# Two transformer layers on one core: earlier loads ahead of attention, idle steps and bursts in the fronts, dummy matmuls at the start

## The chip, the core and the metric

The kernel runs on one NeuronCore of a Trainium2 chip. The metric is the device time of one execution in microseconds (us). A core has TensorE (PE, matmuls; its weight loads are listed apart as PEld), VectorE (DVE), ScalarE (ACT), GpSimd (POOL) and SyncE (SP), each with an instruction stream of its own that runs in order. Streams wait for one another by semaphores. DMA transfers are issued here from SP's stream and, a few, from ACT's; an issue that must wait for data holds up everything behind it in that stream.

## What is computed

Two identical layers, each an attention block and an MLP, over 2048 rows of 640 numbers, 32 heads of 20, 1536 hidden units, all in float32:

```python
def _A_ref(x, wqkv, wo):
    q, k, v = split of x @ wqkv into 32 heads of 20
    p = softmax(einsum("bhqd,bhkd->bhqk", q, k) * 20 ** -0.5)
    return (p @ v, heads joined) @ wo

def _B_ref(x, w1, b1, w2, b2):
    h = relu(x @ w1 + b1)
    return (h * h) @ w2 + b2

x = A_x
for _ in range(2):
    x = x + _A_ref(_layernorm(x), A_wqkv, A_wo)
    x = x + _B_ref(_layernorm(x), B_w1, B_b1, B_w2, B_b2)
```

## The kernel before

**Numbers in two parts.** Operands of the projections are split in a high and a low part of PE's fast float32 format (`F32R`), and each product is three matmuls: high by high, high by low, low by high (`THREE`, L325). The high part is a cast, the low part a subtraction. `split_to` (L256) does this on ACT and DVE, `split_on_pool` (L261) copies on ACT and splits on POOL.

**Stages of a layer.** `layer` (L1223) runs `qkv`, then `attention`, then four row blocks through the output projection and the MLP. A row block is 512 rows (`NQB` = 4 blocks).

**Fronts.** `front` (L438) is a generator: it loads the four 128-row tiles of a block, takes their statistics (`stats`, L241: DVE, then two small operations on POOL), normalises them (`normalise`, L253, on DVE), and transposes them on PE (L453), four transposes for each of the five 128-column chunks, each chunk followed by its split into a tile `xnT`. Every `yield` ends one step: rows, four statistics, four normalisings, five transposed chunks, 14 steps. Block 0 of layer 1 has its own `first_front` (L463), whose transposes are L473. In layer 1 the steps of blocks 1 to 3 are pulled by `qkv`, with the next block's rows requested at the last normalising (`fronts`, L493). In layer 2 (`second`, L1276) blocks 0 to 2 are pulled by the last row block of layer 1's MLP, through `side()`, two steps after each of its units of PE work from the eighth on (L1268), and block 3 by layer 2's `qkv`.

**Projections.** `qkv` (L783) goes through 40 units of 15 steps each (`UNITS`: first four column blocks of queries and keys for every row block, then the other six), then 16 value units (`v_unit`, L416) of 30 steps. A step is one full matmul in the first four units (L353) and two half matmuls later (L358 and, 22 steps behind, L367). After every step `between` (L901) counts: every fourth step pulls one step of the fronts, and at a pace written by hand it puts in a pair of score tiles (L561) whose row maxima DVE takes (L587 for plain ones; L595 on ACT and L602 on DVE for two tiles at once). These maxima are needed before the softmax. `STEPS` and `DOUBLE` say after which unit which maxima are asked for; `tiles` (L827) loads the keys and queries of an item and of the two after it. Results go to memory as `d_qk` and `d_v`, and come back regrouped by heads: one `load_k` or `load_q` is six DMAs of 80 KB (`load_k` of a kept tile two more, from the constant `d_one`). Stores are issued 10 to 16 steps late (`later`, L820), the value stores 12.

**Around the end of `qkv`** all loads stand in SP's stream in the order in which the code reaches them. After value unit 12 come k(0,0) to k(0,3) and q(1); after unit 13 k(3,0) to k(3,3), q(12) and q(13). k(g,c) is the c-th quarter of the keys of the g-th group of four heads, q(t) the queries of block t = 4g + row block.

**Attention.** `attention` (L985) runs 32 blocks of 16 tiles of 128 keys. `ORDERS` writes out by hand how scores (L657), exponentials on ACT (L664), remaining maxima (L561, from block 12 on) and the products with the values (L669) alternate on PE. For each block the maxima are turned into two rows, stored and loaded beside q (`mrows`, `mrows_load`, L634).

**Buffers.** 42 slots of 4 KB per partition (`slot`, L67) hold all large tiles, a smaller pool the row tiles; the eight PSUM banks are handed out in rings (`ps_q` has five). `sums_t` and `d_one` hold constants; `sums_t` is used once, at the end of each layer's attention (L695).

Of the kernel before, what the change touches and what calls it, by code (L numbers as in the profile page):

```python
# [39 lines left out]
def tile_layers(  # L40
# [397 lines left out]
    def front(tb, x_src, bank):  # L438

        rows = [row_tile(x_src, tb * 4 + i) for i in range(4)]  # L440
        yield
        mvs = []
        for x in rows:
            mvs.append(stats(x))
            yield
        for x, mv in zip(rows, mvs):
            normalise(nc.vector, x, mv)
            yield
        res = []
        for k in range(KD):  # L450
            dst = bank("xt")
            for i in range(4):
                nc.tensor.transpose(  # L453
                    dst[:, i * P : (i + 1) * P], rows[i][:, k * P : (k + 1) * P], ident
                )
            t = slot([P, 2, QB], F32R, "xnT")
            (split_on_pool if tb > 1 else split_to)(t[:, 0, :], t[:, 1, :], dst)
            res.append(t)
            if k == KD - 1:
                xt_[tb] = res  # L460
            yield

    def first_front(x_src):  # L463


        rows = [row_tile(x_src, i) for i in range(4)]
        yield
        mvs, dsts = [], [ps_all("xt") for _ in range(KD)]

        def turn(i):  # L470
            normalise(nc.vector, rows[i], mvs[i])
            for k in range(KD):
                nc.tensor.transpose(  # L473
                    dsts[k][:, i * P : (i + 1) * P], rows[i][:, k * P : (k + 1) * P], ident
                )

        for i in range(4):
            mvs.append(stats(rows[i]))
            if i:
                turn(i - 1)  # L480
            yield
        turn(3)
        yield
        res = []
        for dst in dsts:
            t = slot([P, 2, QB], F32R, "xnT")
            split_to(t[:, 0, :], t[:, 1, :], dst)
            res.append(t)
            if len(res) == KD:
                xt_[0] = res  # L490
            yield

    def fronts(steps):  # L493


        for n, f in enumerate(steps):
            for m, _ in enumerate(f):
                if m == 7 and n + 1 < len(steps):
                    next(steps[n + 1])
                yield  # L500

# [281 lines left out]
    def qkv(first, x_src, rest):  # L783
# [22 lines left out]
        for k in range(KD if first else w_v.n):  # L806
            n = len(UNITS) - 7 + k
            if first:
                at(early, n - 2, lambda k=k: raws.append(raw_rows(wqkv[:, 2 * D :], k)))
                at(late, n, lambda k=k: w_v.put(  # L810
                    raws.pop(0), k * 4, k * 4 + 2, 2, nc.scalar.copy, pool_lo
                ))
            else:
                at(early, len(UNITS) - 4 + k // 2, lambda k=k: w_v.load(k))

        def begin(when, n):
            for f in when.pop(n, ()):
# [83 lines left out]
        def between(cost):  # L901
            state["pace"] -= cost
            if state["pace"] <= 0:
                state["pace"] += some()
            settle(state["n"])
            state["n"] += 1
            if state["n"] % 4 == 0:
                next(rest, None)

        run = Halves(between)  # L910
# [24 lines left out]
        for tt in range(NKT):  # L935

            def end(store, tt=tt):
                later(store, 12)
                if tt % 4 == 3:
                    del xt_[tt // 4]  # L940

            v_unit(tt, run, end)
            if first:
                w_v.save_full(1)
            if tt == 10:
                load_v(0, 0)
            if tt == 12:
                for c in range(4):
                    assert (0, c) not in k_t
                    load_k(0, c, True)  # L950
                load_q(1)
            if tt == 13:
                for c in range(4):
                    load_k(3, c, True)
                for qb in range(2):
                    load_q(3 * NQB + qb)
        while run.behind:
            run.catch()
        while double or twos or begun:
# [263 lines left out]
    def layer(first, x_a, x_m, x_e, front_0, ahead):  # L1223
        qkv(first, x_a, front_0)
        if first:
            dma(nc.sync, b1_t, b1.rearrange("(f p) -> p f", p=P))
            dma(nc.sync, b2_t, b2.partition_broadcast(P))
        xs = []
        attention(first, x_a, xs)
        steps = []  # L1230
# [28 lines left out]
        for qb in range(NQB):  # L1259
# [5 lines left out]
                steps.extend([None] * 6 + [step, both, both, step, step, step, step, both])  # L1265
            elif ahead:
                some = lambda: [next(ahead, None) for _ in range(2)]
                steps.extend([None] * 7 + [some] * 21)  # L1268
            xnt = mlp(qb, xnt, x_m, x_e, side, rows if qb + 1 < NQB else None)
            if qb + 1 < NQB:  # L1270
                all_steps()
# [15 lines left out]
    def begin_first():  # L1287
        f = first_front(x_in)
        next(f)
        for pos in range(FIRST):  # L1290
            raws.append(raw_cols(wqkv, ORDER[pos]))
        steps = [front(tb, x_in, ps_q) for tb in (1, 2, 3)]
        for _ in range(5):
            next(f)
# [8 lines left out]

    ones = slot([2, QB], F32, "ones")
    nc.vector.memset(ones, 1.0)
    for p in range(2):
        dma(nc.scalar, d_one[:, p, :], ones)
    for h in range(4):
        r = 32 * h + DH
        dma(nc.scalar, sums_t[r : r + 1, 32 * h : 32 * h + 32], d_one[0, :1, :32])  # L1310
    ahead = second()
    layer(True, x_in, d_x[0], d_x[1], begin_first(), ahead)
    layer(False, d_x[1], d_x[2], x_out, ahead, None)
# [28 lines left out]
```

## Time and profile before

| | us |
|---|---|
| median of 3 runs | 3647.99 |
| lowest and highest | 3645.79, 3652.98 |
| the profiled execution, its own time | 3648.68 |
| its span, first to last instruction | 3646.9 |
| PE busy | 3589.5 |
| ACT busy | 2701.7 |
| DVE busy | 2648.6 |
| POOL busy | 865.5 |

The rows quoted below come from one profiled execution. Times run from the start of the span. Line numbers are those of the kernel before. A row of the timeline has start, length, engine, line, operation, what it writes and reads, the count where equal instructions were merged, and in brackets how long the engine stood before it and for what. A row of waits has the waiting work, what it waited for, the sum, the number of times and the longest. A row of windows has the window, its length, then the busy time and the number of instructions of PE, PEld, DVE, ACT and POOL, then the clock that the throttle granted PE (1.00 is full), the DMA engines' busy share and GB/s.

In this execution layer 1's `qkv` fills the time to about 348, its attention that to 1415, its output projection and MLP that to 1841; in layer 2 the same borders lie at about 2160 and 3233.

### The profile page before, as it was taken

What the parts mean: (1) busy time and instruction counts of PE and PEld (TensorE: products, weight loads), DVE (VectorE), ACT (ScalarE), POOL (GpSimd) and SP (SyncE); (2) the same over time, 40 slices, a digit from 0 to 9 for tenths busy, and PEclk for the clock granted to TensorE, in tenths of its full rate; (3) what the DMA queues carried; (4) which work ended last, traced back from release to release, by engine and by line L of the source; (5) the groups of instructions that cost most, each with busy time, mean ns of one, the idle gap of its engine ahead of it and who ended that gap; (6) DMA issues with size and microseconds to landing.
All of it is one profiled execution on the core that took longest, in us unless ns stands there. A gap on an engine that the chain in (4) does not pass through costs nothing.

```text
span 3646.9 us, 70099 instructions
## 1 busy us (share of the span) xinstructions
PE 3589.5 (98%) x25492; PEld 2180.7 (60%) x25492; DVE 2648.6 (73%) x5208; ACT 2701.7 (74%) x5330; POOL 865.5 (24%) x993
## 2 busy tenths in 40 slices
PE   8999999999999999999999999999999999999999
PEld 5998433333343435989889973343343434368998
DVE  7998888888888871445569988888888888615543
ACT  2888999999999995122228879999999999942221
POOL 6540234322112211112163201221122112201210
PEclk9999999999999999999999999999999999999999
DMA  7665454432222136622357552222222121365221
GB/s 228 230 226 175 123 165 143 138 97 78 58 55 56 53 96 208 245 73 73 102 181 228 180 170 72 72 73 59 77 74 56 47 61 51 101 224 220 73 80 37
DMA packets 282793, 433.79 MB, mean 119 GB/s; under 512 B 71188, under 2 KB 130324, under 8 KB 282448
## 3 DMA queue, kind: packets, MB, share of 16 engines
q1 hardware_dynamic: 281904, 427.60, 37.7%
q8 instruction: 202, 3.31, 0.4%
q10 hardware_dynamic: 544, 1.71, 0.2%
q14 instruction: 143, 1.17, 0.1%
HBM read 284.48 MB, written 144.68 MB: 118 GB/s over the span
## 4 chain that ended last, share of the span: by engine, by line
PE 92%; DMA 3%; DVE 2%; ACT 2%; POOL 1%; issue 0%; SPq 0%; ACTq 0%; POOLq 0%; DVEq 0%
PE banks L669 27%; PE banks L338 21%; PE banks L657 20%; PE banks L561 14%; PE banks L367 5%; PE banks L358 4%; DMA k<-d_qk 1%; ACT e L664 1%; DMA d_qk<-ev 0%; DMA q<-d_qk 0%; SPq L76 0%; PE banks L453 0%; DVE h L259 0%; DVE r L1191 0%; ACT h L258 0%
## 5 line engine op out<-in xcount | busy, mean ns | idle before, releaser
L664 ACT ACTIVATE e<-banks 128x512 f32<-128x512 f32 x4096 | 2075.6, 616 | 57.5 <-PE banks L657 23.4
L573 DVE TENSOR_REDUCE mx<-banks 128x1 f32<-128x512 f32 x2560 | 1619.6, 685 | 354.2 <-PE banks L561 313.5
L657 PEld LDWEIGHTS banks<-q,k 62*128 62x128 f32 x4096 | 573.7, 184 | 895.9 <-ACT e L664 823.5
L669 PE MATMUL banks<-e,vg 128*32 128x512 f32 x8192 | 1093.9, 606 | 11.6 <-ACT e L664 11.6
L657 PE MATMUL banks<-q,k 62*128 62x512 f32 x4096 | 1086.1, 444 | 1.1 <-ACT e L664 1.1
L561 PE MATMUL banks<-k,q 60*128 60x512 f32 x3392 | 990.5, 413 | 11.1 <-DMA q<-d_qk 9.0
L561 PEld LDWEIGHTS banks<-k,q 60*128 60x128 f32 x3392 | 499.4, 186 | 108.3 <-DVE mx L573 71.1
L602 DVE CUSTOM_DVE_ANT_0 rl<-banks,rl 128x512 f32<-128x512 f32 x704 | 456.4, 688 | 25.8 <-PE banks L561 6.7
L595 ACT ACTIVATE rl<-banks 128x512 f32<-128x512 f32 x704 | 382.0, 601 | 58.5 <-PE banks L561 43.1
L338 PE MATMUL banks<-w,h 128*128 128x320 f32 x2304 | 349.3, 311 | 2.7 <-DVE h L259 2.5
L669 PEld LDWEIGHTS banks<-e,vg 128*32 128x32 f32 x8192 | 161.3, 108 | 313.2 <-issue 260.8
L1190 ACT ACTIVATE r<-banks,b_t 128x512 f32<-128x512 f32 x96 | 66.1, 689 | 379.0 <-PE banks L338 208.3
L338 PEld LDWEIGHTS banks<-w,h 128*128 128x128 f32 x2304 | 339.3, 188 | 11.4 <-DVE h L259 6.4
L367 PE MATMUL banks<-xnT,wqk 64*128 64x512 f32 x1080 | 331.4, 396 | 1.6 <-DVE turned_t L360 1.6
L338 PE MATMUL banks<-xnT,w 128*128 128x512 f32 x1440 | 331.6, 391 | 0.0
L358 PE MATMUL banks<-xnT,wqk 64*128 64x512 f32 x1080 | 328.7, 396 | 0.0
L338 PEld LDWEIGHTS banks<-xnT,w 128*128 128x128 f32 x1440 | 270.7, 189 | 55.7
L713 POOL TENSOR_TENSOR few<-few,minus_t 128x16 f32<-128x16 f32 x62 | 179.8, 2900 | 220.0 <-DMA few<-d_s 212.2
L724 POOL TENSOR_TENSOR o<-o 128x512 f32<-128x512 f32 x62 | 79.5, 1282 | 595.9 <-DMA o<-d_r 282.2
L367 PEld LDWEIGHTS banks<-xnT,wqk 64*128 64x128 f32 x1080 | 202.6, 188 | 12.9 <-DVE turned_t L360 2.1
L561 PE MATMUL banks<-kd,q 60*128 60x512 f32 x704 | 208.4, 397 | 1.2 <-ACT rl L595 1.2
L358 PEld LDWEIGHTS banks<-xnT,wqk 64*128 64x128 f32 x1080 | 200.1, 188 | 11.6 <-issue 2.6
(88 smaller groups left out, 2729.5 us busy)
## 6 DMA issues: line engine op xcount, KB each, us to landing
q<-d_qk SPq DMA_DIRECT2D x888, 80.0 KB
d_qk<-ev SPq DMA_DIRECT2D x80, 512.0 KB
k<-d_qk SPq DMA_DIRECT2D x456, 80.0 KB
x<-d_x SPq DMA_DIRECT2D x96, 320.0 KB
d_o<-ot SPq DMA_DIRECT2D x248, 80.0 KB
ot<-d_o SPq DMA_DIRECT2D x38, 512.0 KB
d_v<-v SPq DMA_DIRECT2D x32, 512.0 KB
vg<-d_v SPq DMA_DIRECT2D x32, 512.0 KB
```

The source lines that it names most:

```text
L338: nc.tensor.matmul(dst, a, b, start=(n == 0), stop=(n == last))
L358: nc.tensor.matmul(dst, a[:64], b[:64], start=start, stop=last)
L367: nc.tensor.matmul(dst, a, b, start=False, stop=last, skip_group_check=True)
L561: nc.tensor.matmul(dst, q_t[t][b : b + 60, p, sub * P : (sub + 1) * P], k_t[t // NQB, c][b : b + 60, p, :], start=True, stop=True,)
L573: nc.vector.tensor_reduce(maxima(t)[:, 2 * p + par, sub, c : c + 1], dst, axis=AX.X, op=ALU.max)
L595: nc.scalar.activation(r, dst, AF.Relu)
L602: nc.vector.tensor_tensor_reduce(out=r[par], in0=dst, in1=r[par], scale=1.0, scalar=LEAST, op0=ALU.add, op1=ALU.max, accum_out=maxima(t)[: ...
L657: nc.tensor.matmul(dst, k_t[t // NQB, kt // 4][b : b + 62, p, (kt % 4) * P : (kt % 4 + 1) * P], q_t[t][b : b + 62, p, :], start=True, stop ...
L664: nc.scalar.activation(es[p][:, par, :], dst, AF.Exp, scale=SCALE)
L669: nc.tensor.matmul(acc[32 * h : 32 * h + 32, :], v_t[t // NQB, kt // 8][:, kt % 8, 32 * h : 32 * h + 32], es[p][:, par, :], start=(kt == 0 ...
L713: nc.gpsimd.tensor_tensor(few, few, minus_t, op=ALU.pow)
L724: nc.gpsimd.tensor_mul(o[:, 0, :], o[:, 0, :], o[:, 1, :])
```

## The change

- `front`: one step without work after the statistics and one after the normalisings; the five chunks are transposed in two bursts, of three and two chunks, each followed by its splits. 13 steps in place of 14. The request for the next block's rows stays at the last normalising.
- `between`: a step of the fronts every 3 steps while the count is below 60, every 4 from there, in both layers.
- Layer 2's fronts beside the MLP: 19 times two steps and once one, in place of 21 times two.
- `first_front`: dummy matmuls of the identity with itself into a bank that nothing reads: 11 ahead of the statistics, 3 behind the transposes of each of the first three row tiles, 6 behind the fourth.
- Value weights of layer 2 are loaded one unit earlier.
- Keys and queries for attention: k(0,0), k(0,1) after value unit 8, k(0,2), k(0,3) after 9, k(3,0) and q(12) after 11, k(3,1) to k(3,3) after 12, q(1) and q(13) after 13.
- The two stores of `d_one` move from ACT's stream at the start to SP's, behind the raw weights; the four loads of `sums_t` move from ACT's stream at the start to SP's after layer 1's `qkv`.

```diff
@@ front
+        yield
         for x, mv in zip(rows, mvs):
             normalise(nc.vector, x, mv)
             yield
+        yield
         res = []
-        for k in range(KD):
-            dst = bank("xt")
-            for i in range(4):
-                nc.tensor.transpose(
-                    dst[:, i * P : (i + 1) * P], rows[i][:, k * P : (k + 1) * P], ident
-                )
-            t = slot([P, 2, QB], F32R, "xnT")
-            (split_on_pool if tb > 1 else split_to)(t[:, 0, :], t[:, 1, :], dst)
-            res.append(t)
-            if k == KD - 1:
+        for ks in (range(3), range(3, KD)):
+            dsts = [bank("xt") for _ in ks]
+            for k, dst in zip(ks, dsts):
+                for i in range(4):
+                    nc.tensor.transpose(
+                        dst[:, i * P : (i + 1) * P], rows[i][:, k * P : (k + 1) * P], ident
+                    )
+            for k, dst in zip(ks, dsts):
+                t = slot([P, 2, QB], F32R, "xnT")
+                (split_on_pool if tb > 1 else split_to)(t[:, 0, :], t[:, 1, :], dst)
+                res.append(t)
+            if len(res) == KD:
                 xt_[tb] = res
             yield
+    def warm(n):
+        for _ in range(n):
+            nc.tensor.matmul(banks[:, 0, :P], ident, ident, start=True, stop=True)
@@ first_front
-
+            warm(6 if i == 3 else 3)
+
+        warm(11)
         for i in range(4):
             mvs.append(stats(rows[i]))
@@ fronts
-                if m == 7 and n + 1 < len(steps):
+                if m == 8 and n + 1 < len(steps):
@@ qkv
-                at(early, len(UNITS) - 4 + k // 2, lambda k=k: w_v.load(k))
+                at(early, len(UNITS) - 5 + k // 2, lambda k=k: w_v.load(k))
...
-            if state["n"] % 4 == 0:
+            if state["n"] % (3 if state["n"] < 4 * 3 * KD else 4) == 0:
                 next(rest, None)
...
-            if tt == 12:
-                for c in range(4):
+            if tt in (8, 9):
+                for c in (0, 1) if tt == 8 else (2, 3):
                     assert (0, c) not in k_t
                     load_k(0, c, True)
+            if tt == 11:
+                load_k(3, 0, True)
+                load_q(3 * NQB)
+            if tt == 12:
+                for c in range(1, 4):
+                    load_k(3, c, True)
+            if tt == 13:
                 load_q(1)
-            if tt == 13:
-                for c in range(4):
-                    load_k(3, c, True)
-                for qb in range(2):
-                    load_q(3 * NQB + qb)
+                load_q(3 * NQB + 1)
@@ layer
         if first:
...
+            for h in range(4):
+                r = 32 * h + DH
+                dma(nc.sync, sums_t[r : r + 1, 32 * h : 32 * h + 32], d_one[0, :1, :32])
...
-                steps.extend([None] * 7 + [some] * 21)
+                steps.extend([None] * 7 + [some] * 19 + [lambda: next(ahead, None)])
@@ begin_first
+        for p in range(2):
+            dma(nc.sync, d_one[:, p, :], ones)
@@ tile_layers
-    for p in range(2):
-        dma(nc.scalar, d_one[:, p, :], ones)
-    for h in range(4):
-        r = 32 * h + DH
-        dma(nc.scalar, sums_t[r : r + 1, 32 * h : 32 * h + 32], d_one[0, :1, :32])
```

## The prediction, made before the result was known

> **What bounds the kernel.** First the busy times, then the chain that ended last, then TensorE's (PE's) own waits by cause.
>
> ```profile
> PE 3589.5 (98%) x25492; PEld 2180.7 (60%) x25492; DVE 2648.6 (73%) x5208; ACT 2701.7 (74%) x5330; POOL 865.5 (24%) x993
> ...
> PE 92%; DMA 3%; DVE 2%; ACT 2%; POOL 1%; issue 0%; SPq 0%; ACTq 0%; POOLq 0%; DVEq 0%
> ```
> ```profile
> PE banks L453 <- DVE x L254: 9.9, 11, 2.2
> PE banks L561 <- DMA q<-d_qk: 9.0, 6, 4.8
> ...
> PE banks L358 <- DMA wv<-d_wv: 2.0, 2, 1.6
> ```
>
> PE is the bound: busy 98% and 92% of the chain, so an edit pays only where PE stands still or runs at a reduced clock. Span 3646.9 less 3589.5 busy leaves 57 us of standing; three causes above hold 21 us of it, and the change touches all three. What follows a stand is dearer than the stand, as the windows by stage show (PE busy is the second figure, the granted clock the third from the end):
>
> ```profile
> 348.00:363.00 15.00, 12.04 (x58) 4.52 (x55) 5.46 (x10) 9.04 (x19) 0.46 (x2) 0.77 0.65 226
> ...
> 2160.00:2178.00 18.00, 12.41 (x58) 4.55 (x55) 5.24 (x10) 8.80 (x18) 0.46 (x2) 0.72 0.63 204
> ```
>
> These are the entries into attention of layer 1 and of layer 2: PE busy 12.0 of 15 and 12.4 of 18 us, and that at 0.77 and 0.72 of full clock. The profiled execution took 3648.7 us, 0.7 over the median of the runs shown (3648.0); I sum against it.
>
> **The change, part by part.** (A, B) **The loads moved to earlier steps of the values' projections.** Layer 1's entry, on PE and on ScalarE (ACT):
>
> ```profile
> 347.72 0.50 PE L657 MATMUL banks<-q,k 62*128 62x512 f32 x1
> ...
> 352.69 0.76 PE L561 MATMUL banks<-k,q 60*128 60x512 f32 x1 [2.24 <-DMA q<-d_qk]
> ...
> 363.02 1.07 PE L669 MATMUL banks<-e,vg 128*32 128x512 f32 x8
> ...
> 385.70 1.06 PE L669 MATMUL banks<-e,vg 128*32 128x512 f32 x8
> ```
> ```profile
> 348.81 3.05 ACT L664 ACTIVATE e<-banks 128x512 f32<-128x512 f32 x6
> ```
>
> The first score is at 347.72. The first product with the values (L669, four heads) needs four exponentials, done at 348.81 + 4 x 3.05/6 = 350.85; say it starts at 351.1, 3.4 after the first score. From the fourth L669 (363.02) to the fifteenth (385.70) are 11 tiles of keys, 2.06 us each. Without the wait for q the fourth is due at 351.1 + 3 x 2.06 = 357.3: 5.7 us earlier. In layer 2:
>
> ```profile
> 2159.74 0.50 PE L657 MATMUL banks<-q,k 62*128 62x512 f32 x1
> ...
> 2167.28 0.76 PE L561 MATMUL banks<-k,q 60*128 60x512 f32 x1 [4.79 <-DMA q<-d_qk]
> ...
> 2178.27 1.06 PE L669 MATMUL banks<-e,vg 128*32 128x512 f32 x8
> ```
>
> The same 3.4 and three tiles put the fourth L669 (2178.27) at 2169.3: 9.0 earlier. Are the loads early enough? SyncE's (SP's) queue in layer 2:
>
> ```profile
> 2101.81 7.21 SPq L76 DMA_DIRECT2D d_v<-v  x2
> ...
> 2129.49 0.61 SPq L76 DMA_DIRECT2D k<-d_one  x2
> ...
> 2162.24 5.74 SPq L76 DMA_DIRECT2D q<-d_qk  x12
> ```
>
> From 2129.5 to 2168.0 SP issues eight k and three q without a pause: 38.5/11 = 3.5 us for each load, by issue and not by bandwidth. The row at 2101.81 shows SP standing 7 us for a value store not yet computed. Such stores come once per step, 6.8 us apart (an estimate from 7.21 for two, one of which is the wait). At steps 8 and 9 two loads each (7.0 us) fill one such gap; at 11 two more; three at 12 (10.5) overrun by 4; two at 13 then end near 2147, some 13 us before the first score. In the new order k(3,0) and q(12), which the first maxima read, come before what is needed later. The loads of q for the maxima of the projections are pushed back by at most 7 us; they are asked for two items ahead, an item being 8 x 2 pairs of tiles. I take 8.5 of 9.0 in layer 2 (ends 4 and 9.0).
>
> In layer 1 the four copies into sums_t now stand in SP's queue at this entry. On ACT they were
>
> ```profile
> 4.78 5.08 ACTq L76 DMA_DIRECT2D sums_t<-d_one  x4
> ```
>
> four issues over 5.08 us, one waiting for the other. Behind them on SP stand q(2), k(1,0) and the rows of maxima for block 1:
>
> ```profile
> 353.55 3.16 SPq L76 DMA_DIRECT2D d_v<-v  x4
> 361.70 0.37 SPq L76 DMA_DIRECT2D vg<-d_v  x1
> ...
> 375.85 5.12 SPq L76 DMA_DIRECT2D q<-d_m  x8
> ```
>
> The four value stores stood behind the q loads; vg follows the last by 5.0 (361.70 - 356.7). With SP free the last store can go when its values are there (ACT copies them ahead of 348.81), at about 349.4, and vg at 354.4: 7.3 earlier. Less 5.1 for the copies, the rows go out at 374 to 379 and land near 381. Block 1's first score, now just ahead of the fifteenth L669 (385), would be due at 379.3: a new wait of some 2 us, with PE's whole queue behind it. So 5.7 - 2.0 = **3.7** (ends 2.0 and 5.7). The d_one copies on SP put off the next x rows by two issues; DVE reaches these rows only after it has split xnT, which covers that.
>
> (C) **Value weights one unit earlier in layer 2.** PE waits 2.0 for them, and the clock falls to 0.74:
>
> ```profile
> 2048.00:2050.00 2.00, 0.55 (x3) 0.56 (x5) 0.00 (x0) 0.00 (x0) 0.42 (x1) 0.74 0.84 324
> ```
>
> One unit is 15 steps, some 4 us with the maxima between (15 x 0.2305 x 1.2), but SP is in order and loads of kd, k and q stand ahead of the last weights. I take **1.7**, between 0 and 3.2 (2.0 and about 1.2 at the low clock).
>
> (D) **Idle steps and bursts in layer 2's fronts beside the MLP.** Transposes stand directly behind the normalising of their last row (DVE, VectorE):
>
> ```profile
> 1781.53 0.33 PE L453 MATMUL banks<-ident,x 128*128 128x128 f32 x1 [0.78 <-DVE x L254]
> ...
> 1788.64 17.29 PE L338 MATMUL banks<-xnT,w 128*128 128x512 f32 x75
> ...
> 1806.61 0.33 PE L453 MATMUL banks<-ident,x 128*128 128x128 f32 x1 [0.56 <-DVE x L254]
> ...
> 1809.63 0.33 PE L453 MATMUL banks<-ident,x 128*128 128x128 f32 x1 [2.17 <-DVE x L254]
> 1809.72 5.27 PE L338 MATMUL banks<-xnT,w 128*128 128x512 f32 x15
> ```
>
> The added steps put one unit of the MLP between them and the normalising, 15 matmuls at 17.29/75 = 0.2305 us = 3.5, more than the 2.17. The first front stands 0.78, and the third, which lies alike, as much; the second stands 0.56 + 2.17, and then 15 matmuls take 5.27 instead of 3.46, 1.8 lost at the low clock. 0.78 x 2 + 2.73 - 0.2 left + 1.8 = **5.9** (ends 3.3 and 6.1: one stand and most of the clock's part stay, or nothing is left).
>
> (E) **The last front of layer 2** lies in the projections, one step every 3 matmuls instead of 4.
>
> ```profile
> 1845.72 0.89 DVE L246 BATCH_NORM_STATS2 bst<-x 128x6 f32<-128x320 f32 x2 [5.03 <-DMA x<-d_x]
> ...
> 1853.76 0.33 PE L453 MATMUL banks<-ident,x 128*128 128x128 f32 x1 [0.73 <-DVE x L254]
> ```
>
> Its x rows are the MLP's last store; DVE stood 5.03 for them, and the last transpose of the first group went at 1853.76. The burst stands at count 36, the first group stood at 40: PE asks 4 matmuls (0.9) sooner for rows that come no sooner, and the third front's last transposes (about 1 us), which lay behind the last store, lie ahead of it now. Less work on GpSimd beside the normalising gives some back. **-1.0** (ends -2.6 and 0).
>
> (F) **Fronts in layer 1.** Maxima and fronts share DVE:
>
> ```profile
> 52.17 1.29 DVE L587 TENSOR_REDUCE mx<-banks 128x1 f32<-128x512 f32 x2 [0.55 <-PE banks L561]
> 53.38 0.88 DVE L246 BATCH_NORM_STATS2 bst<-x 128x6 f32<-128x320 f32 x2
> ...
> 62.49 0.60 DVE L254 TENSOR_SCALAR x<-x,mv 128x640 f32<-128x640 f32 x1
> ```
> ```profile
> 50.36 0.66 PE L453 MATMUL banks<-ident,x 128*128 128x128 f32 x4
> ...
> 79.26 0.66 PE L453 MATMUL banks<-ident,x 128*128 128x128 f32 x4
> ```
>
> From the last transposes of block 2 (end 51.0) to those of block 3 (79.9) are 52 steps of the matmul count: 52 x 0.2305 + 12 pairs of maxima x 0.2305 + 5 x 0.66 = 18.1 us of PE work in 28.9. Lost: 10.8. I count the steps of the projections (one matmul or one pair of halves each); the maxima begin at about 75. Before, block 2's statistics lie at 56 to 68 and its transposes at 88 to 104, block 3's at 108 to 120 and 140 to 156. With a step every 3 up to 60 and the new idle steps and bursts, block 2's statistics lie at 39 to 48, ahead of the maxima, and its bursts at 72 and 76; block 3's at 80 to 92, its bursts at 120 and 124. A pair of maxima takes DVE 1.2 for 1.15 of PE, so DVE has no room: block 3's front, 4 x 1.0 + 4 x 0.6 = 6.4 us, must still be paid, less the two pairs that PE may run ahead in five banks (2.4): 4.0 lost, in pieces of under 1.2. With 0.8 at block 2's burst, 10.8 - 4.8 = **6.0** (ends 0: it only moves; 10: it hides).
>
> (G) **Dummy matmuls and ACT freed at first.**
>
> ```profile
> 9.90 1.35 ACT L161 CAST wqk<-raw 128x640 fp32r<-128x640 f32 x2 [7.68 <-DMA sums_t<-d_one]
> ```
> ```profile
> 13.70 9.35 PE L353 MATMUL banks<-xnT,wqk 128*128 128x512 f32 x31 [0.79 <-DVE xnT L259]
> 23.56 1.21 PE L353 MATMUL banks<-xnT,wqk 128*128 128x512 f32 x4 [0.52 <-POOL wqk L273]
> ```
>
> ACT stood 7.68 in its queue, but the chain that ended last reaches this cast from the raw weights' landing and not from the queue, so freeing it gives some tenths at most. The 31 matmuls took 9.35 for 7.15: 2.2 lost cold. The 26 dummies cover that, and run where PE waits for DVE. If one takes as long as two transposes (2 x 0.66/4 = 0.33, an estimate), the six behind the last row hold back the first projection by 2.0, of which DVE's split of xnT hides most; without that cover it is the lower end. But at 23.56 PE stands for POOL's split of weights, and with four statistics' steps by count 12 POOL reaches that split later. **0** (ends -2 and 2.2).
>
> Sum: 8.5 + 3.7 + 1.7 + 5.9 - 1.0 + 6.0 + 0 = 24.8; 3648.7 - 24.8 = **3623.9**.
>
> The Trainium skill, "TensorE: Matmul & The Clock Gate", section "HAM oscillation — how this bites in real kernels", puts the loss of the clock at idle gaps over some 3.4 us. By that, layer 1's entry, whose longest wait is 2.24, would not owe its low clock to this wait. The trace so far disagrees: 0.77 over that stage, and 1.00 again once PE runs. What would follow is rival (5).
>
> **The rivals.** (1) **DVE becomes the bound in the fronts.** For it: 2.00 of 2.00 busy below; against: DVE has idle pieces such as 0.55 ahead of the maxima at 52.17. Then F is 0 and E -2.6: 3648.7 - 17.2 = **3631.5**.
>
> ```profile
> 58.00:60.00 2.00, 0.81 (x8) 0.33 (x4) 1.97 (x6) 0.58 (x1) 1.92 (x4) 1.00 0.54 162
> ...
> 68.00:70.00 2.00, 0.26 (x1) 0.18 (x1) 2.00 (x4) 0.00 (x0) 1.26 (x1) 0.81 0.12 45
> ```
>
> (2) **SP still stands behind the value stores**, so that the moved loads go out only half as early: A 4, B 1: 24.8 - 7.2 = 17.6, **3631.1**. For it the row at 2101.81; against, that the k rows are long stored by then. (3) **The clock falls over the whole stretch of F**, as PE now stands a little at every step. At 40% busy (58 to 60) it was still 1.00, at 13% (68 to 70) 0.81; I expect some 65%. If it falls to a half, 52 counts and 12 pairs cost 0.19 more each, 12 in all, and F is -6; with one such stretch of 3 us in D, 24.8 - 15 = 9.8, **3638.9**. [...] (4) **Slower: no free buffer at step 8.** The arena has 42 slots; by the code the two blocks of xnT left (10), value weights (7), values (4), q (5), k and kd (6) and one vg make 33, and the moves add 4 by step 9 and 2 at 11: close, and decided at 43. Then SP stands at the first moved load until the last projection (2109 to 2160, 51 us), with the maxima's q behind it; those 45 us or so of maxima come alone after it, in each layer, A and B lost: 3648.7 - 12.6 + 90 = **3726**. (5) **The low clock of layer 1's entry stays**, because something else than the wait takes it. Then B loses all but the wait's 2.24, 3.5 us: 24.8 - 3.5 = 21.3, **3627.4**. Against it stands that both entries show the wait and then the clock, and that the stand of 68 to 70 shows the same.
>
> **How the numbers follow.** Forecast 0.57; (1) 0.16; (2) 0.09; (3) 0.08; (4) 0.06; (5) 0.04. The upper ends of all terms give 36.2, so 3612.5 at best; I take 3613. The range goes up past (1), (2) and (5), and with the better part of (3) to 3637; that leaves out (4) and the rest of (3). About 0.2%, 7.3 us, is what a measurement here can tell from no change (the runs of before lie 7.2 apart). Faster: 0.57 + 0.16 + 0.09 + 0.04 + half of (3) 0.04 = 0.90; the worse half of (3) within 0.2%: 0.04; slower: 0.06.
>
> **What would show it.** A, B: no PE wait for q at either entry, clock 1.00 there, last moved load issued before the last value store; a wait of the first score of block 1 for rows of maxima in layer 1. C: the value weights' wait under 1 us. D: no wait for L254 beside the MLP. E: one longer wait for L254 near 1850. F: PE and DVE both near full from 40 to 75, last transposes of block 3 some 10 us earlier in the count. G: the first 31 matmuls in 7.2 us, and a later wait for the weights' split. The prediction is wrong if SP stands for a buffer in the values' projections, or if the clock falls between 40 and 62.

## The result, and the profile after

| | before | after |
|---|---|---|
| median, us (4 runs each) | 3650.48 | 3632.83 |
| lowest and highest | 3645.79, 3655.69 | 3629.56, 3635.37 |
| profiled execution, its own time | 3648.68 | 3631.19 |
| its span | 3646.9 | 3629.4 |

The ratio is 0.9951, with a 95% interval from 0.9933 to 0.9968: 0.5% faster, 18 us by the medians and 17.5 by the spans. Forecast were 24.8. Lines below the insertions have other numbers in the changed kernel: L453 is L456, and L561, L587, L657, L664 and L669 are 11 higher. The page of the changed kernel first, busy times and chain, then PE's waits by cause:

```profile
PE 3583.3 (99%) x25544; PEld 2185.9 (60%) x25544; DVE 2646.8 (73%) x5208; ACT 2701.3 (74%) x5330; POOL 864.1 (24%) x993
...
PE 92%; DVE 2%; DMA 2%; ACT 1%; POOL 1%; SPq 1%; issue 1%; DVEq 0%; POOLq 0%; ACTq 0%
```
```profile
PE banks L353 <- POOL wqk L273: 3.6, 1, 3.6
PE banks L456 <- DVE x L254: 3.2, 4, 1.1
PE banks L572 <- DMA q<-d_qk: 3.1, 1, 3.1
...
PE banks L358 <- DMA wv<-d_wv: 2.5, 1, 2.5
...
PE banks L572 <- DMA raw<-in_A_wqkv_dram: 1.9, 1, 1.9
```

The three causes that held 21 us hold 8.8 now: the normalising (L254) 3.2 for 9.9, q 3.1 for 9.0, and the value weights 2.5 for 2.0. But two of these rows are new in what they stand for. The wait for q is a single one of 3.1, not at an entry into attention but at 86; and 3.6 for GpSimd's split of weights stood at 0.5 before.

Where the 17.5 came from is read by pairing the nth matmul of each kind in the two traces. The changed kernel at the places that part the stages:

```profile
35.26 1.42 PE L358 MATMUL banks<-xnT,wqk 64*128 64x512 f32 x5
...
349.24 0.50 PE L668 MATMUL banks<-q,k 62*128 62x512 f32 x1
...
383.51 1.06 PE L680 MATMUL banks<-e,vg 128*32 128x512 f32 x8
...
1831.48 1.77 PE L353 MATMUL banks<-xnT,wqk 128*128 128x512 f32 x7
...
1853.75 3.71 PE L358 MATMUL banks<-xnT,wqk 64*128 64x512 f32 x15
...
2150.52 0.50 PE L668 MATMUL banks<-q,k 62*128 62x512 f32 x1
...
2160.55 1.06 PE L680 MATMUL banks<-e,vg 128*32 128x512 f32 x8
```

Before, the same instructions started at these times (those of layer 1's and layer 2's first score, fifteenth and fourth product stand in the prediction: 347.72, 385.70, 2159.74, 2178.27):

```profile
33.64 1.65 PE L358 MATMUL banks<-xnT,wqk 64*128 64x512 f32 x6
...
1840.79 1.40 PE L353 MATMUL banks<-xnT,wqk 128*128 128x512 f32 x5
...
1862.01 2.36 PE L358 MATMUL banks<-xnT,wqk 64*128 64x512 f32 x9
```

The differences, from one place to the next, are the terms of the forecast's sum. The last column is a kernel of the experiments (a step of the fronts every 4 throughout), paired with before in the same way; its profiled execution, 3617.24, is the fastest of its four runs (median 3620.42).

| term | stretch up to | forecast | changed kernel | step every 4 |
|---|---|---|---|---|
| G | first L358 | 0 | -1.6 | -0.2 |
| F | first score, layer 1 | 6.0 | 0.1 | 5.4 |
| B | fifteenth product | 3.7 | 3.7 | 5.3 |
| D | layer 2's first projection | 5.9 | 7.1 | 7.2 |
| E | layer 2's first L358 | -1.0 | -1.0 | 3.2 |
| C | first score, layer 2 | 1.7 | 1.0 | 2.0 |
| A | fourth product | 8.5 | 8.5 | 8.5 |
| | end | | -0.2 | |
| sum | | 24.8 | 17.6 | 31.4 |

A, B and E came at their forecast size, D 1.2 above. F gave nothing, and it is here that the trace has to be read closely. It is not that TensorE failed to gain: the 97th first half matmul from unit 4 on went at 79.84 before and goes at 74.58 now, 5.3 earlier. The 135th went at 91.09 and goes at 93.21, 2.1 later.

```profile
79.84 0.50 PE L358 MATMUL banks<-xnT,wqk 64*128 64x512 f32 x1
...
91.09 0.40 PE L358 MATMUL banks<-xnT,wqk 64*128 64x512 f32 x1
```
```profile
74.58 0.39 PE L358 MATMUL banks<-xnT,wqk 64*128 64x512 f32 x1
...
93.21 0.62 PE L358 MATMUL banks<-xnT,wqk 64*128 64x512 f32 x1
```

In between TensorE stands in the changed kernel, and runs at half the clock afterwards; rows of its PE timeline and of its windows (the third figure from the end is the clock):

```profile
86.44 0.47 PE L572 MATMUL banks<-k,q 60*128 60x512 f32 x1 [3.12 <-DMA q<-d_qk]
88.78 0.76 PE L572 MATMUL banks<-k,q 60*128 60x512 f32 x1 [1.87 <-DMA raw<-in_A_wqkv_dram]
```
```profile
84.00:87.49 3.49, 0.47 (x1) 0.18 (x1) 0.55 (x1) 0.00 (x0) 0.00 (x0) 1.00 0.87 159
87.49:90.91 3.42, 2.13 (x10) 1.90 (x12) 0.84 (x2) 0.91 (x2) 0.26 (x1) 0.50 0.92 262
90.91:94.32 3.41, 3.41 (x18) 2.86 (x18) 2.16 (x4) 0.30 (x1) 3.27 (x4) 0.50 0.67 151
```

Standing takes 3.1 + 1.9 = 5.0; from 88.8 to 94.3 TensorE works at half the clock, and half of these 5.5 us, 2.8, is lost. The second row names a load of raw weights, which this matmul does not read (`banks<-k,q`); SP issued it right behind the six parts of q, and the semaphore events of the trace have the last part of q landing at 88.4, just ahead of the matmul. So I read both stands as stands for q. The keys and queries that the maxima wait for were asked for late. SP's stream, and what POOL does at that time:

```profile
65.26 9.58 SPq L76 DMA_DIRECT2D d_qk<-ev  x2
77.74 0.36 SPq L76 DMA_DIRECT2D d_kd<-kd  x1
78.19 2.61 SPq L76 DMA_DIRECT2D k<-d_qk  x6
80.85 3.17 SPq L76 DMA_DIRECT2D q<-d_qk  x6
```
```profile
62.83 0.61 POOL L270 CAST xnT<-r 128x512 fp32r<-128x512 f32 x1 [2.01 <-ACT r L265]
...
71.21 1.29 POOL L273 TENSOR_TENSOR xnT<-r,xnT 128x512 fp32r<-128x512 f32 x1
72.44 0.62 POOL L270 CAST ev<-r 128x512 fp32r<-128x512 f32 x1
...
76.43 1.29 POOL L273 TENSOR_TENSOR kd<-kf,kd 128x512 fp32r<-128x512 f32 x1
```

SP holds a store of ev for 9.6 us and a store of kd until 77.7, and k and q come behind them. These results of unit 6 are computed on POOL, and POOL first does ten instructions without a pause, 62.83 to 72.50: the five splits of block 3, whose bursts the faster steps have put ahead of unit 6's end.

### The profile page after: what moved, and what is told of

Read it like the earlier page. It is cut to its first block, busy times and chain, and to the rows that moved or that the text cites. A ratio compares the mean times of both kernels' runs of the same rounds, so it can differ in the third digit from the quotient of the medians.

```text
span 3629.4 us, 70207 instructions
## 1 busy us (share of the span) xinstructions
PE 3583.3 (99%) x25544; PEld 2185.9 (60%) x25544; DVE 2646.8 (73%) x5208; ACT 2701.3 (74%) x5330; POOL 864.1 (24%) x993
## 4 chain that ended last, share of the span: by engine, by line
PE 92%; DVE 2%; DMA 2%; ACT 1%; POOL 1%; SPq 1%; issue 1%; DVEq 0%; POOLq 0%; ACTq 0%
PE banks L680 27%; PE banks L338 21%; PE banks L668 19%; PE banks L572 14%; PE banks L367 5%; PE banks L358 4%; ACT e L675 1%; DVE mx L598 1%; SPq L76 1%; DMA x<-in_A_x_dram 0%; PE banks L456 0%; PE banks L353 0%; DMA d_qk<-ev 0%; DVE bst L246 0%; DVE h L259 0%
## 5 line engine op out<-in xcount | busy, mean ns | idle before, releaser
L613 DVE CUSTOM_DVE_ANT_0 rl<-banks,rl 128x512 f32<-128x512 f32 x704 | 456.7, 688 | 24.1 <-PE banks L572 4.1
L358 PE MATMUL banks<-xnT,wqk 64*128 64x512 f32 x1080 | 328.1, 396 | 0.0
L358 PEld LDWEIGHTS banks<-xnT,wqk 64*128 64x128 f32 x1080 | 201.1, 188 | 8.7 <-issue 1.0
```

What stands on the lines that cost most here:

```text
L358: nc.tensor.matmul(dst, a[:64], b[:64], start=start, stop=last)
L613: nc.vector.tensor_tensor_reduce(out=r[par], in0=dst, in1=r[par], scale=1.0, scalar=LEAST, op0=ALU.add, op1=ALU.max, accum_out=maxima(t)[: ...
```

## The experiments

**Theory 1**: the steps every 3 put block 3's five splits on GpSimd in one piece ahead of unit 6's keys; SP, in order, holds the next keys and queries behind these; TensorE stands 5.0 and loses 2.8 to the clock. **Theory 2** (the forecast's rival 1; in the expectation of e2 the number stands for another rival): VectorE is the bound in the fronts, and a stand that goes comes back as a stand for maxima. Gains below are (1 - ratio) x 3650 against the runs of before on the same chip; the interval stands with the ratio. The changed kernel has 17.9 (11.7 to 24.5). The intervals reach 3 to 6 us to each side, so the ratios alone do not settle a difference of a few us between two of these kernels.

| kernel | median | ratio (95%) | gain, us |
|---|---|---|---|
| e1 loads alone | 3635.18 | 0.9952 (0.9938, 0.9965) | 17.5 |
| e2 fronts alone | 3647.46 | 0.9990 (0.9981, 0.9998) | 3.7 |
| e3 start alone | 3652.21 | 1.0004 (0.9995, 1.0013) | -1.5 |
| e4 block 3's bursts later | 3624.85 | 0.9928 (0.9916, 0.9940) | 26.3 |
| e5 weights first | 3629.80 | 0.9946 (0.9932, 0.9959) | 19.7 |
| e6 casts on ScalarE | 3625.19 | 0.9934 (0.9922, 0.9947) | 24.1 |
| e7 step every 4 | 3620.42 | 0.9920 (0.9907, 0.9934) | 29.2 |
| e8 four mends | 3620.50 | 0.9922 (0.9909, 0.9934) | 28.5 |
| e9 every 4, no idle steps | 3632.90 | 0.9957 (0.9944, 0.9969) | 15.7 |
| e10 every 4, chunk by chunk | 3618.26 | 0.9919 (0.9905, 0.9932) | 29.6 |
| e11 every 4, two mends | 3619.06 | 0.9915 (0.9901, 0.9928) | 31.0 |
| e12 as e10, no dummies | 3624.40 | 0.9932 (0.9918, 0.9945) | 24.8 |

**The parts by themselves.** e1 is the kernel before with the two hunks on loads (value units 8 to 13, and the value weights), e2 with those on `front`, the pace, `m == 8` and the 19 + 1 steps, e3 with `warm` and the moved d_one and sums_t.

> The kernel before with the moved loads of keys, queries and value weights alone (A, B, C). By the milestones of the traces, layer 1's entry is worth 4.0, layer 2's 8.3 and the value weights 0.5: 12.8 us faster than before. Rival: part of this was owed to the copies into sums_t and to the fronts' new order; then under 9.

> The kernel before with the idle steps, the bursts and the step every 3 matmuls alone (D, E, F). By the milestones D is worth 6.5 and E -1.2, the same here. For F, theory 1 (GpSimd takes block 3's five splits in one piece, ahead of the results of unit 6, so that SyncE holds keys and queries and TensorE stands for them near 84): the stand of some 5 us and the half clock behind it are here as well, F is +1, and all is 6 us faster than before. Rival, theory 2 (the fault lies in the start, which shifts everything by 3): no such stand, F is 6, and all is 11 faster.

> The kernel before with the dummy matmuls and the moved stores of d_one and loads of sums_t alone (G). The projections run warm, then TensorE stands for GpSimd's split of weights. Theory: with three statistics ahead of that split instead of four the stand is about 2.2 instead of 3.65; from 1 us slower to 1 us faster than before. Rival: the dummies themselves cost what they take, 3 us slower.

17.5 + 3.7 - 1.5 = 19.7, and the changed kernel's 17.9 lies within what the intervals allow: whether the parts help or hinder each other can't be told from the times. **The loads alone can't be told from the whole change.** e1 was expected at 12.8; its ratio gives 17.5 (12.8 to 22.6), its span 13.5 (3633.4 for 3646.9). e2's stand for q and raw is there without any change at the start, so theory 1's rival (the start shifts it) falls:

```profile
PE banks L565 <- DMA q<-d_qk: 2.9, 1, 2.9
...
PE banks L565 <- DMA raw<-in_A_wqkv_dram: 1.2, 1, 1.2
```

e2's 3.7 (0.7 to 6.9) lies below the 6 expected, though the interval reaches it. By its trace D is worth 7.0 there too and F is -2.3 (+1 expected), but TensorE then stands 4.1 for the value weights instead of 2.0, since they land no sooner: what D gains is kept only with the earlier loads of C (2.5 in the changed kernel). e3 (-1.5, from -4.7 to 1.8) can be told neither from no change nor from the 3 us slower of its rival; its stand for the weights' split is 2.4, near the 2.2 expected.

**The stand at 84.** Two ways to take it away, on the changed kernel. e4 lets the order of the work change, e6 lets the order stay and shortens GpSimd's part:

```diff
@@ e4, ahead of the bursts
+        if tb == 3 and x_src is x_in:
+            yield
+            yield
@@ e6
+                if tb == 3:
+                    r = xtile("r")[:, :QB]
+                    nc.scalar.copy(r, dst)
+                    nc.scalar.copy(t[:, 0, :], dst)
+                    pool_lo(t[:, 1, :], r, t[:, 0, :].bitcast(F32))
+                else:
                     (split_on_pool if tb > 1 else split_to)(t[:, 0, :], t[:, 1, :], dst)
```

> The changed kernel with two more idle steps ahead of the bursts of layer 1's block 3, so that GpSimd gets unit 6's result ahead of the block's five splits. Theory 1: the stand for keys and queries near 84 (3.1 and 1.9 us) and the half clock behind it (5.2 us at a half, 2.6 lost) go: 5 to 8 us faster than the changed kernel. Rival, theory 2: VectorE owes the maxima anyway, and TensorE stands for them instead; under 2 us faster.

> The changed kernel with the high parts of block 3's transposed rows cast on ScalarE instead of GpSimd, in both layers; the order of the work stays. It takes 5 x 0.67 = 3.4 us from GpSimd ahead of unit 6's result. Theory 1 (GpSimd's time ahead of that result sets the stand): the keys and queries are asked for 3 us sooner, the stand of 5.0 near 84 falls to about 2, and 3 to 5 us are gained on the changed kernel. Rival (the place of the bursts in the order matters, not GpSimd's time): no change.

e4: 26.3 for 17.9, 8 more by the ratios, 4.7 by the spans (3624.7 for 3629.4). SP's stream and the window of the stand in e4; POOL now does unit 6's keys ahead of the splits, and they are stored at 70.8:

```profile
70.81 0.36 SPq L76 DMA_DIRECT2D d_kd<-kd  x1
72.16 2.21 SPq L76 DMA_DIRECT2D k<-d_qk  x6
```
```profile
80.00:90.00 10.00, 10.00 (x90) 8.15 (x88) 10.00 (x20) 2.39 (x4) 9.51 (x12) 1.00 0.55 160
```

k is asked for 6.0 us sooner, TensorE is busy 10.00 of 10 at full clock, and VectorE too: the stand did not come back as a stand for maxima within it, but VectorE has no room left there. In e6 the wait for q falls to 0.3, the one behind it stays at 1.7:

```profile
PE banks L578 <- DMA q<-d_qk: 0.3, 1, 0.3
```

With the order unchanged k is asked for 2.0 us sooner (3 expected), and the two stands fall from 5.0 to 2.0: GpSimd's time ahead of unit 6's keys sets the stand. Theory 1 holds for it, and its rivals fall. Less of it is left further on. The trace of e4 is 6.7 ahead of the changed kernel's at 95 and 4.2 at 230, that of e6 5.2 and 1.5. What takes the rest back in e4 is not VectorE, as theory 2 would have it, but ScalarE's part of the maxima and a load of kd:

```profile
PE banks L575 <- ACT rl L609: 1.4, 1, 1.4
PE banks L575 <- DMA kd<-d_kd: 1.1, 1, 1.1
```

e6 stands 1.1 for kd as well, and the clock is a half from 109.2 to 112.6. So most of e6's 6 us is not owed to the stand: its casts moved in layer 2 too, and there C is 4.1 for 1.0, with 0.3 of standing for the value weights in place of 2.5.

**The pace.** e7 is the changed kernel with one line back:

```diff
-            if state["n"] % (3 if state["n"] < 4 * 3 * KD else 4) == 0:
+            if state["n"] % 4 == 0:
```

> The changed kernel with a step of the fronts every 4 matmuls throughout, bursts and idle steps kept. By theory 1 block 3's bursts then come at counts 148 and 152, behind unit 6's result: no stand for keys and queries near 84; three statistics stand ahead of the weights' split, so its stand is about 2.2; but the fronts of blocks 2 and 3 lie beside the maxima as before, so that TensorE stands for VectorE between 56 and 75 as in the kernel before. Net 0 to 4 us faster than the changed kernel. Rival: the step every 3 carries the gain of the fronts, and without it the time is 3 to 6 slower.

I expected 0 to 4 on the changed kernel, and it is 11 (13.9 by the spans, 3615.5 for 3629.4): the largest gain of one edit on the changed kernel. Up to 6.8 of the 13.9 is the clock's: TensorE's clock is a half for 20.5 us in the changed kernel's trace and for 6.8 in e7's. By the table of stages it gives 1.4 at the start, 5.3 in F, 4.2 in E. All that the idle steps and bursts were forecast to give in F is there (5.4 for 6.0), and nothing of it needed the step every 3. My expectation that TensorE stands between 56 and 75 as before was half right (PE is busy 7.18 of 10 us from 60 to 70), but these stands are paid in any case. In layer 2 the burst now comes at count 48, when the rows are nearly normalised. This row of e7's waits is that front alone:

```profile
PE banks L456 <- DVE x L254: 1.4, 3, 1.0
```

1.4 us of standing in all, and a clock of 1.00; the changed kernel stands 2.8 there, and then runs at a half:

```profile
1840.85 0.33 PE L456 MATMUL banks<-ident,x 128*128 128x128 f32 x1 [1.03 <-DVE x L254]
1842.32 1.00 PE L456 MATMUL banks<-ident,x 128*128 128x128 f32 x2 [1.14 <-DVE x L254]
1843.97 2.18 PE L456 MATMUL banks<-ident,x 128*128 128x128 f32 x9 [0.65 <-DVE x L254]
```
```profile
1844.00:1848.00 4.00, 4.00 (x16) 3.60 (x17) 0.00 (x0) 1.76 (x3) 2.71 (x4) 0.50 0.65 231
```

**Idle steps or bursts.** Both are e7 with one thing more:

```diff
@@ e9, twice in front; with m == 7, and 16 + 1 steps beside the MLP
-        yield
@@ e10, one chunk a step where the front lies in the projections
-        for ks in (range(3), range(3, KD)):
+        for ks in [[k] for k in range(KD)] if bank is ps_q else (range(3), range(3, KD)):
```

> The changed kernel with a step every 4 throughout and without the idle steps: bursts alone. Theory: the idle steps let the normalising end before TensorE comes to the transposes; without them TensorE stands directly behind it again in each front (0.8 to 2.7 us in each of three beside the MLP, the same in layer 1 and the last), so the time is 4 to 8 us above that of the step every 4 with idle steps. Rival: the bursts carry the gain (one stand in place of several); within 3.

> The changed kernel with a step every 4 throughout, with the idle steps, and in the fronts that lie in the projections (layer 1's three, layer 2's last) one chunk for each step instead of bursts. The last transposes of block 3 come 12 counts later. Theory: idle steps carry the gain of F; within 3 us of the step every 4 with bursts. Rival: the bursts carry it, by bringing the transposed rows sooner and by fewer banks held among the maxima; 4 to 8 above.

Without the idle steps 13 us are lost, more than the 4 to 8 expected. By the traces of e7 and e9 it is 15.7: 8.7 in F, D and E, where the fronts lie, 3.5 in C, and 3.1 at the entries B and A, where e9's clock falls. The stands for the normalising are back (3.7 us in layer 2's fronts, in 7 pieces, for 1.4 in e7), and, where 11 steps in place of 13 bring block 3 sooner, so is a stand for keys and queries near 86 (2.4). Without the bursts nothing is lost. **The idle steps carry the gain of the fronts**, as far as these edits part it: e9 also brings block 3 sooner, and the stand near 86 belongs to that. The bursts do neither good nor harm where they were tried; beside the MLP they weren't tried apart.

```profile
PE banks L454 <- DVE x L254: 3.7, 7, 0.8
```

**The start.** e5 is the changed kernel with the first hunk below. e8 has both hunks, e4's two steps in layer 1 and four such steps in layer 2. e11 is e7 with both hunks.

```diff
-                at(late, n, lambda pos=pos: w_qk.put(
+                at(late if pos >= FIRST else early, n, lambda pos=pos: w_qk.put(
@@ value weights
-                at(early, len(UNITS) - 5 + k // 2, lambda k=k: w_v.load(k))
+                at(early, len(UNITS) - 5 + k // 3, lambda k=k: w_v.load(k))
```

> The changed kernel with the weights of positions 2 and 3 split one unit earlier on ScalarE and GpSimd, ahead of the statistics of block 1. Theory: the fourth statistic that the step every 3 puts ahead of this split is what makes TensorE stand 3.65 us at 24.83 and run at 0.76 of full clock behind it; the stand falls under 1 us, and the projections reach unit 4 some 4 us sooner. Of this at most 4 us are left at the end, since VectorE is the bound from 48 to 64. Rival: the dummy matmuls only bring TensorE sooner to the same VectorE work; nothing is left at the end.

> The changed kernel with four mends: layer 1's bursts of block 3 two steps later, the first weights split one unit earlier, the last value weights loaded with the unit before, layer 2's bursts of block 3 four steps later (there TensorE stands 2.8 for the normalising and runs at a half for some 5 us). By the theory the gains add: 5 to 8, 0 to 4, 2.5 and 3 to 5, in all 11 to 18 us on the changed kernel. Rival (VectorE and GpSimd are full and the stands only move): under 9.

> The changed kernel with a step every 4 throughout, the first weights split one unit earlier, and the last value weights loaded with the unit before. Theory: the stand of 2.4 for the weights goes, and the 1.9 for the value weights; block 1's transposes come at count 45 rather than 36, so that VectorE's normalising is done and the clock stays at 1.00 there; 3 to 6 us below the step every 4 alone. Rival: TensorE comes too early for VectorE again, stands in small pieces and runs at a half for 10 us and more, as it did between 36 and 48 with the weights first and a step every 3; no gain.

e5's start comes 3.4 to 4.2 sooner, as expected, and all of it is gone by 45; its 19.7 can't be told from the changed kernel's 17.9. The trace shows to what: TensorE now comes to block 1's burst ahead of VectorE, stands in pieces of 0.6 and 0.8 us, and runs at half the clock from 35.1 to 48.8.

```profile
35.32 0.48 PE L456 MATMUL banks<-ident,x 128*128 128x128 f32 x1 [0.79 <-DVE x L254]
36.38 2.18 PE L456 MATMUL banks<-ident,x 128*128 128x128 f32 x9 [0.59 <-DVE x L254]
```
```profile
34.00:36.00 2.00, 1.00 (x4) 0.46 (x3) 1.55 (x4) 0.00 (x0) 1.60 (x3) 0.78 0.68 172
```

e8 has the same piece of low clock; its gain of 10.6 on the changed kernel lies between what the theory asked for (11 to 18) and its rival (under 9), and is no more than e7 has with one edit. e11 gains nothing that can be measured over e7: the weights' and the value weights' stands are gone, but TensorE comes sooner to keys and queries that are still on their way (1.3 us at 36.59) and its clock is a half from 36.8 to 43.6, much as its rival had it (10 us and more).

e12 is e10 without the dummy matmuls:

```diff
-            warm(6 if i == 3 else 3)
-        warm(11)
```

> The kernel of the run before last with a step every 4, idle steps and chunk by chunk, without the dummy matmuls (the moved stores of d_one and loads of sums_t stay). Theory: cold, the first 31 projections take 9.35 instead of 7.2, and the stand for GpSimd's split of weights shrinks from 2.4 to about 0.5 in return; within 2 us of that kernel. Rival: the dummies also save the low clock behind that stand (0.83 from 20 to 30); 3 to 5 slower.

24.8 for 29.6: nearer to the rival (3 to 5 lost) than to no effect, but the intervals overlap, and by the traces only some 3 us of the difference lie before 80. The clock is a half for 17.1 us in e12's trace and for 3.4 in e10's. What the dummies are worth stays open between 0 and 5.

The fastest kernels, e7, e8, e10 and e11, beat both the kernel before (by 28 to 31 us) and the changed one (by 11 to 13; each of their runs, the highest 3625.4, lies below the lowest of the changed kernel, 3629.56), and can't be told from one another.

## Why the prediction was right, and where it was not

**A** (8.5 forecast, 8.5 measured) failed at no step: SP fits two loads in each gap between value stores, no wait for q is left at layer 2's entry, and the clock is 1.00 there. That the clock holds is in part luck: of the eleven kernels with these loads, e4, e5, e8, e9 and e11 have a half clock for 3.4 to 6.8 us at this entry, and A is 6.7 to 7.4 by their traces.

```profile
2150.00:2168.00 18.00, 17.44 (x117) 7.85 (x117) 12.18 (x22) 16.26 (x33) 0.92 (x4) 1.00 0.38 118
```

**B** (3.7 and 3.7) has the right sum from two wrong terms that cancel. The copies into sums_t take 1.4 us on SP, not the 5.1 that the row of ACT's stream gave (there each stood for something else), so there is no new wait for rows of maxima. But the low clock did not go with the wait: it falls to a half from 354 to 357 behind a stand of no more than 0.6.

```profile
356.24 1.43 SPq L76 DMA_DIRECT2D sums_t<-d_one  x4
```
```profile
348.00:363.00 15.00, 14.44 (x87) 6.89 (x89) 7.58 (x15) 11.14 (x23) 0.90 (x4) 0.89 0.55 152
```

(15.00 - 0.56) at 0.89 is 1.6 lost: about half of rival (5). In e7, e8 and e10, which have the same loads, the clock stays at 1.00 through this entry and B is 5.2 to 5.3, so the arrangement does not force it; the last section has what goes with it.

**C** (1.7 and 1.0) lies within its ends, but not by the wait, which was to fall under 1 us: it is 2.5 for 2.0 before. Six of seven loads go sooner, and the last, issued at 2037.65, stands behind kd, k and q, the reason given for the lower end. The 1.0 comes from the clock, which stays at 1.00 here; before, it was a half for 3.4 us from 2049.0. What the loads are worth shows in e2: without them TensorE, which D brings 7 us sooner, stands 4.1.

**D** (5.9 and 7.1) is right in place and mechanism, 1.0 above its upper end; no wait for L254 is left beside the MLP. The waits for L254 that are gone are 4.5 and the half clock before was 3.4 us long (1.7 lost), 6.2 in all; where the other 0.9 come from stays open. Layer 1's attention gave none of it. e9 shows that the idle steps do it.

**E** (-1.0 and -1.0) is right in sign and size. One longer wait was to show it; TensorE stands 2.8 in three pieces, for 2.6 in four before, and what grew more is the time at a half, 6.8 us for 3.4, which the forecast did not count. The same reasoning should have been turned round: rows that come no sooner want later steps, and with a step every 4 the term is +3.2.

**G** (0 and -1.6) is within its ends, and the wait came as named, a fourth statistic on GpSimd ahead of the weights' split. The 2.2 won by warm projections were paid back by a stand of 3.65 and by 3.4 us at half the clock behind it. With a step every 4 it is -0.2.

**F** (6.0 and 0.1) is the step that failed. The forecast counted VectorE's work against TensorE's, count by count, and took the bound from these two. It moved the transposes of block 3 from counts 140 to 156 up to 120 and 124, and never asked what each burst issues on the other engines: five splits, 9.7 us of GpSimd, ahead of unit 6's keys at 127, and behind these SP's stream. The part up to 80 came as forecast (5.3 ahead, 7 from unit 4 on), with the 4.0 that VectorE was to keep: from 48 to 64 VectorE is busy 15.8 of 16 us, TensorE 12.0. The stand of 5.0 and the clock's 2.8 took it back.

So the likeliest case of the forecast was not the one that happened. The median lies 8.9 above it (the profiled execution 7.3), inside the range, near that of rival (1) (3631.5). But rival (1) was to come from VectorE, and e4 and e6, which leave VectorE's work as it is, take the stand away or cut it to 2.0: the number was near, the mechanism another. That the sum of the other terms held is partly luck too, since A, B, C and E each shift by 1 to 2 us with a piece at half the clock that comes or stays away. Rival (2) did not come (A is whole), nor (4): SP stands for no buffer. Of (3), the low clock over the stretch from 40 to 62, nothing is seen in the changed kernel (1.00 from 36 to 84); it came elsewhere, behind the stands at 24, 86, 354 and 1842.

## What to carry to other kernels

A step that is moved ahead of another engine's work is moved ahead on every queue it feeds: list what it issues on each engine, with the counts, and see whose results then stand behind it, down to the stores and the loads behind those stores. Producers want distance to the consumer, not speed: a step of waiting between the normalising and the transposes gave what faster pulling took away. And undo a change edit by edit even when it is faster in all: here one edit cost 11 us of a possible 29.

## What the runs showed of the hardware

**The clock has two levels and comes in pieces of 3.41 us.** In the clock record of all fourteen traces the granted clock is 1.00 or 0.50 and nothing between, and every stretch at a half that ends within the kernel's work lasts 3.41 us, or two, three or four times that. A 0.77 or 0.89 in a row of windows is the mean of such pieces and of full clock. In e5:

```profile
31.70:35.12 3.42, 2.82 (x13) 1.85 (x11) 3.35 (x9) 0.04 (x1) 3.18 (x6) 1.00 0.88 313
35.12:48.77 13.65, 12.87 (x49) 9.73 (x50) 5.79 (x15) 2.93 (x5) 10.58 (x14) 0.50 0.94 320
48.77:52.18 3.41, 3.41 (x30) 2.87 (x30) 3.38 (x9) 0.51 (x1) 1.33 (x4) 1.00 0.65 199
```

Counted over the fourteen traces in pieces of 3.41 us, laid so that the changes of the clock fall on their borders: each of the 33 pieces at full clock in which TensorE was busy less than 48% was followed by a piece at a half; of 289 pieces between 48% and 86%, 32 were; of 14423 above that, none. In between the busy share does not decide.

At the entries into attention the place of the borders goes with the outcome. The eleven kernels with the moved loads have 22 entries, and 13 of them lose the clock. A border lies 1.4 to 2.1 us behind the first score in 8 of the 9 that keep it, and in none of the 13. This is read off the traces; no run moved the borders on purpose. If it is the cause, part of a kernel's time is chance. Runs of one kernel do differ with the clock: e7's four took 3617.24, 3618.90, 3621.94 and 3622.20 at mean clocks of 0.999, 0.998, 0.997 and 0.996. Up to the last few us of the kernels, TensorE's clock is a half for 34.1 us in the trace of before and for 20.5 in the changed kernel's, so up to 6.8 of the 17.5 won is the clock's.

**Half the clock without a long stand.** In e5 no stand between 34 and 38 exceeds 0.79 us, yet the granted clock is 0.50 from 35.1 to 48.8, with TensorE busy 2.00 of 2 in every window from 38 on; in the changed kernel a single stand of 3.65, which ended at 24.8, was followed by one piece at a half:

```profile
26.05:29.47 3.42, 3.42 (x16) 3.02 (x15) 1.98 (x3) 1.65 (x4) 0.79 (x1) 0.50 0.96 269
```

The Trainium skill, "TensorE: Matmul & The Clock Gate", section "HAM oscillation — how this bites in real kernels", asks for no idle gaps over some 3.4 us; the traces disagree: pieces under 1 us, which leave TensorE busy half of 2 us, were enough. The next section of that page of the Trainium skill, "A second HAM failure mode: psum-queue depth-cycling", has frequent short idling as a second cause, and with that the rows of e5 agree. In the changed kernel's layer 2 entry pieces of 0.5 and 0.6 left the clock at 1.00, so size alone does not decide either.

**The clock's share can exceed the stand's.** 5.0 us of standing at 84 cost 7.8 in all; 1.4 us in two pieces at 35 cost e5 some 6 more (13.7 at a half).
